# Which of the two DMA queues carries which of the first loads: one change to a fused LayerNorm, SSM and SwiGLU kernel

## The chip, the core and the metric

The kernel runs on one core of a Trainium2 chip. Its engines are TensorE (PE in the profile, with PEld for its weight loads), VectorE (DVE), ScalarE (ACT), GpSimd (POOL) and SyncE (SP). SyncE does no arithmetic here: it issues nearly all the DMAs. ScalarE issues a few at the very start. The DMAs of SyncE and those of ScalarE form two queues, and 16 DMA engines move the bytes of both. The metric is the device time of one execution in microseconds; less is better.

## The reference

The input `x` has 2048 rows of 512 bf16 values. It is normalised row by row, and the normalised rows go through two branches whose results are added to `x`:

```python
xn = _layernorm(x, axis=-1)
# branch A: a diagonal complex state-space model, state size 512
Lam_bar = jnp.exp(dt * Lam)
B_bar = ((Lam_bar - 1.0) / Lam)[:, None] * Bmat
Bu = jnp.einsum("bld,pd->blp", xn + 0j, B_bar)
# h_t = Lam_bar * h_(t-1) + Bu_t, for t = 0 .. 2047, kept as hseq
yA = 2.0 * jnp.einsum("blp,dp->bld", hseq, Cmat).real + xn * Dskip
# branch B: SwiGLU with 1376 hidden units
yB = (silu(xn @ w_gate) * (xn @ w_up)) @ w_down
return x + yA + yB
```

## The kernel before, in words

The 2048 rows are 16 tiles of 128 rows, and four tiles make a chunk; there are four chunks. The inner dimension of 512 is four K tiles of 128. For each chunk TensorE multiplies the transposed normalised rows by the gate and up weights and by the SSM input matrix; VectorE runs the recurrence as scans; in the end TensorE accumulates the down projection and the SSM output in the same banks, and VectorE adds them to `x` (`dc_pair`).

The kernel is written as a graph of tasks (`g.add`, and `dma` for transfers). A planner, `_schedule`, orders the tasks of ScalarE, VectorE and GpSimd by estimated times. Tasks of SyncE and TensorE stay in the order in which they were written (`_CHAIN`). The transfers on ScalarE's queue are chained by `order=`, so they are its first instructions. Every DMA has a semaphore of its own, and what needs its bytes waits for that semaphore.

The change is about the first microseconds, the work on chunk 0 (`ln_chunk0`, `xt_tile` and `ffn_gate_quarters`). There, everything is cut finer than later:

- Each of the four `x` tiles is loaded by a DMA of 128 KB (`x_load`), and each K tile of the first seven gate column blocks (896 of 1376 columns) by a DMA of 224 KB (`wg_load`; the names of its four DMAs end in k0 to k3).
- For each `x` tile VectorE takes the statistics (`bn_stats`, L518, and `bn_aggr`, L519), ScalarE the square root (L520), VectorE the reciprocal (L525) and the normalised tile (L501). TensorE transposes the tile into PSUM (L549), and ScalarE copies the result to SBUF in pieces (L560); VectorE does so for the last tile (L558).
- TensorE then multiplies by quarters (L764): for `x` tile 0, seven matmuls of 128 columns with K tile 0, seven with K tile 1, seven with K tile 2 and seven with K tile 3; then the same for `x` tiles 1, 2 and 3. The two transposes of the first half of `x` tile 1 stand after the fourth matmul of K tile 2. TensorE takes all this in the written order, so a K tile that is missing holds up everything behind it.
- Before the data arrive TensorE runs matmuls on a constant (`pe_warm`, L480).

SyncE's queue begins with `x` 0, `x` 1, gate k1, `x` 2, gate k3, `x` 3; then come three small parameter rows (`pload`) and the large loads of the up weights, of the remaining gate columns and of `x` tiles 4 to 7. ScalarE's queue begins with `ld_touch`, a read of 16 pairs of elements, one pair from every eighth row of gate K tile 0, whose destination `tch` nobody reads; then gate k0 and gate k2.

Of the kernel before, what the change touches and what calls it, by code (L numbers as in the profile page):

```python
# [12 lines left out]
B16 = mybir.dt.bfloat16  # L13
# [237 lines left out]
def bass_parallel_sum__ssm_conv_s5__swiglu_ffn__prompt_kernel(  # L251
# [23 lines left out]
    KT = D // 128  # L275
# [6 lines left out]
    g = _Graph()  # L282
    es = ExitStack()
    with es:
        def sb(name, shape, dt):
            return es.enter_context(nc.sbuf_tensor(name, shape, dt))
# [7 lines left out]
        x_sb = sb("x_sb", [128, NT, D], B16)  # L294
# [34 lines left out]
        st = sb("st", [128, 8, 6], F32)  # L329
# [4 lines left out]
        mhalf = sb("mhalf", [128, NT], F32)  # L334
        sd0 = sb("sd0", [128, 4], F32)
        epst = sb("epst", [128, 1], F32)
        tch = sb("tch", [16, KT, 2], B16)
        prT = sb("prT", [128, 32], B16)
        praw = prT[:].rearrange("p (a e) -> p e a", e=8)
        prow = sb("prow", [128, 32], B16)  # L340
# [48 lines left out]
        x_v = A_x[0].rearrange("(a p) d -> p a d", p=128)  # L389
        out_v = out[0].rearrange("(a p) d -> p a d", p=128)  # L390
        wg_v = B_w_gate.rearrange("(k p) f -> p k f", p=128)
# [5 lines left out]
        def dma(name, dst, src, writes, nbytes, reads=(), after=(), out_=False, eng="sp", xpose=False, prio=0.0, order=(), beside=(), **kw):  # L397
            after = tuple(after)
            if xpose:
                after = after + tuple(t for t in dma_tasks if t.name not in beside)  # L400
                fn = lambda e, dst=dst, src=src: e.dma_start_transpose(out=dst, in_=src)
                est, nb = 1900.0, int(nbytes * 1.2) + 140000
            else:
                if xp_state[0] is not None:
                    after = after + (xp_state[0],)
                fn = lambda e, dst=dst, src=src: e.dma_start(dst, src, **kw)  # L406
                est, nb = 330.0 + nbytes / 900.0, nbytes
            t = g.add(eng, fn, reads=reads, writes=writes, name=name, dma=True, after=after, out=out_, est=est, nbytes=nb, prio=prio, order=order)
            dma_tasks.append(t)
            if xpose:  # L410
                xp_state[0] = t
            return t

        TILEB = 128 * D * 2
# [7 lines left out]
        def x_load(a, **kw):  # L422
            return dma("ld_x%d" % a, x_sb[:, a:a + 1, :], x_v[:, a:a + 1, :], [("x", a)], TILEB, **kw)

        def wg_load(nm, k0, k1, **kw):
            return dma("ld_wg" + nm, wg[:, k0:k1, 0:FG], wg_v[:, k0:k1, 0:FG], [("wg", nm)], (k1 - k0) * 128 * FG * 2, **kw)

        g.add("pool", lambda e: e.memset(prow[:], 0.0), writes=[("prow0",)], name="prow0", est=100)
        x_load(0)
        x_load(1)  # L430
        act_q = [dma("ld_touch", tch[0:16, 0:1], wg_v[0:128:8, 0:1, 0:2], [("tch",)], 16 * 4, eng="act")]
        act_q.append(wg_load("k0", 0, 1, eng="act", order=(act_q[-1],)))
        act_q.append(wg_load("k2", 2, 3, eng="act", order=(act_q[-1],)))
        wg_load("k1", 1, 2)
        x_load(2)
        wg_load("k3", 3, 4)
        x_load(3)
        pload("ld_ldt", 2, A_log_dt)
# [11 lines left out]
        def loads_stage_b2():  # L450
# [11 lines left out]
              reads=[("dsk",)], writes=[("ident",)], name="ident", est=300)  # L462
        g.add("pool", lambda e: e.iota(iot[:], pattern=[[1, TP]], base=0, channel_multiplier=0, allow_small_or_imprecise_dtypes=True),
              writes=[("iot",)], name="iota", est=1000)
# [35 lines left out]
        def ln_apply(a, order=()):  # L500
            return g.add("dve", lambda e: e.tensor_scalar(out=xn_sb[:, a % NXN, :], in0=x_sb[:, a, :], scalar1=mv[:, a, 0:1], scalar2=rstd[:, a:a + 1],  # L501
                                                          op0=ALU.subtract, op1=ALU.mult),
                         reads=[("x", a), ("mv", a), ("rstd", a)], writes=[("xn", a % NXN)], name="xn%d" % a, est=350, order=order)
# [10 lines left out]
        def ln_chunk0():  # L514
            last = None
            for a in range(4):
                order = (last,) if last else ()
                last = g.add("dve", lambda e, a=a: e.bn_stats(out=st[:, a, :], in_=x_sb[:, a, :]), reads=[("x", a)], writes=[("st", a)], name="bnst%d" % a, est=640, order=order)  # L518
                last = g.add("dve", lambda e, a=a: e.bn_aggr(out=mv[:, a, :], in_=st[:, a, :]), reads=[("st", a)], writes=[("mv", a)], name="bnag%d" % a, est=160, order=(last,))  # L519
                hold["sd%d" % a] = g.add("act", lambda e, a=a: e.activation(out=sd0[:, a:a + 1], in_=mv[:, a, 1:2], func=AF.Sqrt, bias=EPS),  # L520
                                         reads=[("mv", a)], writes=[("sd0", a)], name="sd%d" % a, est=190)
                if a == 3:
                    last = g.add("dve", lambda e: e.transpose(out=prT[:], in_=prow[:]), reads=[("prow", k) for k in range(3)] + [("prow0",)],
                                 writes=[("praw", k) for k in range(3)], name="parT", est=90, order=(last,))
                last = g.add("dve", lambda e, a=a: e.reciprocal(out=rstd[:, a:a + 1], in_=sd0[:, a:a + 1]), reads=[("sd0", a)], writes=[("rstd", a)],  # L525
                             name="rstd%d" % a, est=140, order=(last,))
                last = ln_apply(a, (last,))
            hold["xn3"] = last
# [214 lines left out]
        def ffn_gate_quarters(pairs):  # L743
# [5 lines left out]
            pe_warm(8, 512, wbank)  # L749
            pe_warm(2, 128, wbank)  # L750
            ln_chunk0()
            xt_tile(0, 0, 1, wbank)
            xt_tile(0, 1, 4)
# [309 lines left out]
```

## Time and profile before

| what | us |
|---|---|
| median of three runs | 178.35 (178.0, 178.35, 180.07) |
| profiled execution, its own time | 177.91 |
| its span, from the first to the last instruction | 176.1 |
| PE busy | 172.5 (98%) |
| DVE busy | 162.0 (92%) |
| ACT busy | 83.5 (47%) |
| share of PE in the chain that ended last | 95% |
| share of DMA in that chain | 3% |

The profiled execution spends 1.8 us outside its span. The chain that ended last is followed back from the last instruction, at each step to what released it; what lies on it set the end. Busy times of other engines are no cost of their own.

These are the first DMAs, in the order of their issue. The start of the issue is from the timeline, the time from there to landing from the list of DMA issues, each asked for in a window that holds that issue alone or beside one of another tile; the last column is their sum, to 0.1 us.

| transfer | queue | issue starts | issue to landing | landed |
|---|---|---|---|---|
| touch read | ACT | 0.78 | 1.9 | 2.7 |
| x 0 | SP | 0.79 | 2.1 | 2.9 |
| gate k0 | ACT | 1.23 | 3.2 | 4.4 |
| x 1 | SP | 1.25 | 3.0 | 4.3 |
| gate k2 | ACT | 1.70 | 4.7 | 6.4 |
| gate k1 | SP | 1.71 | 4.47 | 6.18 |
| x 2 | SP | 2.18 | 4.5 | 6.7 |
| gate k3 | SP | 2.66 | 4.5 | 7.2 |
| x 3 | SP | 3.14 | 4.4 | 7.5 |

### The profile page before, as it was taken

What the parts mean: (1) busy time and instruction counts of PE and PEld (TensorE: products, weight loads), DVE (VectorE), ACT (ScalarE), POOL (GpSimd) and SP (SyncE); (2) the same over time, 40 slices, a digit from 0 to 9 for tenths busy, and PEclk for the clock granted to TensorE, in tenths of its full rate; (3) what the DMA queues carried; (4) which work ended last, traced back from release to release, by engine and by line L of the source; (5) the groups of instructions that cost most, each with busy time, mean ns of one, the idle gap of its engine ahead of it and who ended that gap; (6) DMA issues with size and microseconds to landing.
All of it is one profiled execution on the core that took longest, in us unless ns stands there. A gap on an engine that the chain in (4) does not pass through costs nothing.

```text
span 176.1 us, 2524 instructions
## 1 busy us (share of the span) xinstructions
PE 172.5 (98%) x978; PEld 84.8 (48%) x978; DVE 162.0 (92%) x279; ACT 83.5 (47%) x113; POOL 10.8 (6%) x21
## 2 busy tenths in 40 slices
PE   7899999999999999999999999999999999999995
PEld 2794444444444496444444444444444444444443
DVE  2776998899999999999999999999999999999933
ACT  4469989799999866597560000000265620000000
POOL 3040500127000000000000000000000000000000
PEclk9999999999999999999999999999999999999999
DMA  5898663566685202300411000022100000000122
GB/s 165 269 384 184 118 119 113 178 121 103 119 275 128 40 0 60 63 0 2 112 39 28 4 0 0 0 84 98 60 0 0 0 0 0 4 0 0 60 91 89
DMA packets 27143, 13.69 MB, mean 78 GB/s; under 512 B 19356, under 2 KB 27004, under 8 KB 27132
## 3 DMA queue, kind: packets, MB, share of 16 engines
q1 hardware_dynamic: 26812, 13.08, 28.6%
q10 hardware_dynamic: 320, 0.46, 0.8%
q8 instruction: 7, 0.11, 0.3%
q14 instruction: 4, 0.03, 0.1%
HBM read 6.85 MB, written 2.10 MB: 51 GB/s over the span
## 4 chain that ended last, share of the span: by engine, by line
PE 95%; DMA 3%; SPq 0%; issue 0%; DVE 0%
PE pb L721 36%; PE pb L918 20%; PE pb L932 16%; PE pb L849 16%; PE pb L764 3%; PE pb L814 3%; DMA wgu<-in_B_w_gate_dram 3%; PE pb L957 2%; SPq L406 0%; PE pb L549 0%; DVE x_sb L936 0%; PE pb L929 0%
## 5 line engine op out<-in xcount | busy, mean ns | idle before, releaser
L721 PE MATMUL pb<-xnT,wgu 128*128 128x512 bf16 x212 | 46.2, 379 | 0.0
L889 DVE TENSOR_TENSOR_SCAN rot<-sm,car,rot 128x512 bf16<-128x512 f32 x32 | 39.2, 1267 | 0.1
L733 ACT ACTIVATE sg<-pb 128x1024 bf16<-128x1024 f32 x20 | 20.1, 1022 | 39.6 <-PE pb L721 38.4
L721 PEld LDWEIGHTS pb<-xnT,wgu 128*128 128x128 bf16 x212 | 20.7, 98 | 24.8 <-ACT sg L733 0.2
L932 PE MATMUL pb<-W,hss 128*128 128x512 bf16 (+2 forms) x136 | 28.2, 367 | 0.0
L918 PE MATMUL pb<-wd,hT 128*128 128x512 bf16 (+2 forms) x130 | 26.4, 363 | 0.0
L799 ACT ACTIVATE uf<-pb 128x1024 bf16<-128x1024 f32 x20 | 20.5, 1027 | 6.4 <-PE pb L721 5.3
L849 PE MATMUL pb<-xnT,BT 128*128 128x512 bf16 x96 | 21.0, 379 | 0.0
L932 PEld LDWEIGHTS pb<-W,hss 128*128 128x128 bf16 x136 | 12.8, 98 | 15.2 <-issue 0.8
L856 ACT ACTIVATE u_sb<-pb 128x1024 bf16<-128x1024 f32 x16 | 16.4, 1023 | 5.8 <-PE pb L849 5.2
L918 PEld LDWEIGHTS pb<-wd,hT 128*128 128x128 bf16 x130 | 12.3, 98 | 14.0
L721 PE MATMUL pb<-scrC,wgu 128*128 128x512 bf16 x80 | 17.4, 379 | 0.0
L849 PEld LDWEIGHTS pb<-xnT,BT 128*128 128x128 bf16 x96 | 9.4, 98 | 11.3
L936 DVE TENSOR_TENSOR x_sb<-pb,x_sb 128x512 bf16<-128x512 f32 (+2 forms) x17 | 10.7, 644 | 4.0 <-PE pb L932 4.0
L721 PEld LDWEIGHTS pb<-scrC,wgu 128*128 128x128 bf16 x80 | 7.8, 98 | 9.2
L802 DVE TENSOR_TENSOR hT<-sg,uf 128x1024 bf16<-128x1024 bf16 x15 | 10.1, 681 | 0.1
L880 DVE TENSOR_TENSOR rot<-u_sb,cosT 128x2048 bf16<-128x2048 bf16 x8 | 9.8, 1220 | 0.5 <-ACT u_sb L856 0.5
L880 DVE TENSOR_TENSOR rot<-u_sb,sin 128x2048 bf16<-128x2048 bf16 x8 | 9.7, 1217 | 0.0
L880 DVE TENSOR_TENSOR rot<-rot,sin 128x2048 bf16<-128x2048 bf16 x8 | 9.7, 1216 | 0.0
L880 DVE TENSOR_TENSOR rot<-rot,cosT 128x2048 bf16<-128x2048 bf16 x8 | 9.7, 1210 | 0.0
L880 DVE TENSOR_TENSOR hss<-rot 128x2048 bf16<-128x2048 bf16 x8 | 9.6, 1216 | 0.0
L880 DVE TENSOR_TENSOR rot<-rot 128x2048 bf16<-128x2048 bf16 x8 | 9.6, 1216 | 0.0
(85 smaller groups left out, 159.7 us busy)
## 6 DMA issues: line engine op xcount, KB each, us to landing
out_dram<-x_sb SPq DMA_DIRECT2D x15, 128.0 KB, 1.7
x_sb<-in_A_x_dram SPq DMA_DIRECT2D x3, 512.0 KB, 4.6
wd<-in_B_w_down_dram SPq DMA_DIRECT2D x1, 1280.0 KB, 6.3
wgu<-in_B_w_up_dram SPq DMA_DIRECT2D x1, 768.0 KB, 4.9
wgu<-in_B_w_up_dram SPq DMA_DIRECT2D x1, 608.0 KB, 6.9
x_sb<-in_A_x_dram SPq DMA_DIRECT2D x4, 128.0 KB, 3.7
wgu<-in_B_w_gate_dram SPq DMA_DIRECT2D x1, 480.0 KB, 5.8
wgu<-in_B_w_gate_dram ACTq DMA_DIRECT2D x2, 224.0 KB, 4.0
```

What stands on the lines that cost most here:

```text
L721: inst = e.matmul(pbank[0:fs, bk, :].rearrange("p (j t) -> p j t", j=4), lhsT=w[:, kt, i * 128:i * 128 + fs], rhs=xnT[c][:, :, kt, :], sta ...
L733: g.add("act", lambda e: e.activation(out=sg[rows, sl, 0:n, :].rearrange("p a t -> p (a t)"), in_=pair_f32(rows, bk, 512 * n), func=AF.Sil ...
L764: inst = e.matmul(pbank[:, bk, q * 128:(q + 1) * 128], lhsT=wg[:, kt, i * 128:(i + 1) * 128], rhs=xnT[0][:, q, kt, :], start=(kt == 0), st ...
L799: g.add("act", lambda e: e.activation(out=uf[rows, ul, 0:n, :].rearrange("p a t -> p (a t)"), in_=pair_f32(rows, bk, 512 * n), func=AF.Ide ...
L802: g.add("dve", lambda e: e.tensor_tensor(out=hT_pair(c, i0), in0=sg[rows, sl, 0:n, :], in1=uf[rows, ul, 0:n, :], op=ALU.mult), reads=[("sg ...
L849: inst = e.matmul(pbank[:, bk, :].rearrange("p (j t) -> p j t", j=4), lhsT=BT[:, ri, kt, pt * 128:(pt + 1) * 128], rhs=xnT[c][:, :, kt, :] ...
L856: g.add("act", lambda e: e.activation(out=u_sb[:, us].rearrange("p r t -> p (r t)"), in_=pair_f32(slice(0, 128), b0), func=AF.Identity), r ...
L880: tt = lambda out, a, b, op, r, w, nm: g.add("dve", lambda e: e.tensor_tensor(out=out, in0=a, in1=b, op=op), reads=r, writes=w, name="%s_% ...
L889: g.add("dve", lambda e, A0=A0, A1=A1, k=k, ri=ri, pt=pt: e.tensor_tensor_scan(out=A1[:, k, ri, :], data0=rr[:, pt:pt + 1].to_broadcast([1 ...
L918: inst = e.matmul(pbank[:, bk, 0:nc_], lhsT=hT_pair(c, i - i % 2)[:, i % 2, lt * 128:(lt + 1) * 128], rhs=wd[:, i, c0:c0 + nc_], start=(i ...
L932: inst = e.matmul(pbank[:, bk, 0:nc_], lhsT=hss[:, hb, pt, ri, lt * 128:(lt + 1) * 128], rhs=W12[:, ri, pt, c0:c0 + nc_], start=False, sto ...
L936: g.add("dve", lambda e: e.tensor_tensor(out=x_sb[:, a, c0:c0 + nc_], in0=pbank[:, bk, 0:nc_], in1=x_sb[:, a, c0:c0 + nc_], op=ALU.add), r ...
```

## The change

The tile `x` 0 is loaded by two DMAs of 64 rows, the first at the head of SyncE's queue, the second at the head of ScalarE's. The read of 16 pairs and its tile `tch` are gone. Gate k0 stays second on ScalarE's queue; behind it comes `x` 2 in place of gate k2. SyncE's queue is now `x` 0 rows 0 to 63, `x` 1, gate k1, gate k2, gate k3, `x` 3, and then as before. The first `bn_stats` waits for both halves.

```diff
-        tch = sb("tch", [16, KT, 2], B16)
...
-        x_load(0)
+        dma("ld_x0", x_sb[0:64, 0:1, :], x_v[0:64, 0:1, :], [("x", 0)], TILEB // 2)
         x_load(1)
-        act_q = [dma("ld_touch", tch[0:16, 0:1], wg_v[0:128:8, 0:1, 0:2], [("tch",)], 16 * 4, eng="act")]
+        act_q = [dma("ld_x0b", x_sb[64:128, 0:1, :], x_v[64:128, 0:1, :], [("x0b",)], TILEB // 2, eng="act")]
         act_q.append(wg_load("k0", 0, 1, eng="act", order=(act_q[-1],)))
-        act_q.append(wg_load("k2", 2, 3, eng="act", order=(act_q[-1],)))
+        act_q.append(x_load(2, eng="act", order=(act_q[-1],)))
         wg_load("k1", 1, 2)
-        x_load(2)
+        wg_load("k2", 2, 3)
         wg_load("k3", 3, 4)
         x_load(3)
...
-                last = g.add("dve", lambda e, a=a: e.bn_stats(out=st[:, a, :], in_=x_sb[:, a, :]), reads=[("x", a)], writes=[("st", a)], name="bnst%d" % a, est=640, order=order)
+                last = g.add("dve", lambda e, a=a: e.bn_stats(out=st[:, a, :], in_=x_sb[:, a, :]), reads=[("x", a)] + ([("x0b",)] if a == 0 else []), writes=[("st", a)], name="bnst%d" % a, est=640, order=order)
```

The planner's estimates change with it, and two small reorderings follow between about 18 and 23 us: VectorE takes one `tzs` step (L673, 0.69 us) after the next up product's multiplication instead of before it, and ScalarE takes one cosine of four values (L614, 0.29 us) ahead of a sine table and a SiLU instead of behind them. TensorE's order is unchanged.

## The prediction

> **What bounds the kernel now.** I read the chain that ended last first, because only what lies on it can move the end. Its pieces in order of time (start, length, what) around the change:
>
> ```profile
> 1.71 4.47 DMA wgu<-in_B_w_gate_dram
> 6.18 0.14 issue
> 6.32 0.77 PE pb L764 x11
> 7.09 0.11 PE pb L549 x2
> 7.20 0.79 PE pb L764 x13
> ...
> 10.99 2.12 PE pb L764 x38
> 13.11 11.22 PE pb L721 x52
> ```
>
> From 6.32 us on the chain is TensorE alone, to 174.33. The transfer ahead of it is gate k1, issued at 1.71, landed at 6.18. Next I read the waits of TensorE over the whole span (who waited for whom: total, times, longest):
>
> ```profile
> PE pb L480 <- PEq L1048: 0.8, 1, 0.8
> PE pb L549 <- DVE xn_sb L501: 0.5, 1, 0.5
> PE pb L764 <- DMA wgu<-in_B_w_gate_dram: 0.4, 1, 0.4
> ```
>
> There are three: the program's start, the first transposes waiting for normalised tile 0, and K tile 1. After that TensorE never waits. So the change is worth what it moves the point from which TensorE runs dense, and no more, as long as nothing behind begins to wait. Third, the stretches of the beginning (from:to, length, busy time of PE, PEld, DVE, ACT and POOL with counts, granted clock, DMA share, GB/s), to see what limits the transfers:
>
> ```profile
> 2.00:3.00 1.00, 1.00 (x4) 0.38 (x3) 0.10 (x1) 0.81 (x1) 0.15 (x4) 1.00 0.88 209
> 3.00:4.00 1.00, 1.00 (x5) 0.32 (x4) 0.77 (x2) 0.93 (x3) 0.00 (x0) 1.00 1.02 340
> 4.00:5.00 1.00, 0.51 (x8) 0.34 (x6) 0.89 (x3) 0.04 (x1) 0.00 (x0) 1.00 0.99 357
> 5.00:6.00 1.00, 0.82 (x11) 0.42 (x8) 0.66 (x4) 0.90 (x4) 0.00 (x0) 1.00 1.04 376
> 6.50:7.50 1.00, 1.00 (x21) 0.94 (x19) 0.81 (x2) 0.26 (x2) 0.00 (x0) 1.00 0.75 104
> 7.50:8.50 1.00, 1.00 (x22) 1.00 (x19) 0.69 (x4) 0.67 (x4) 0.00 (x0) 1.00 0.85 263
> 8.50:9.50 1.00, 1.00 (x21) 0.97 (x19) 0.88 (x3) 0.29 (x3) 0.00 (x0) 1.00 1.05 389
> ```
>
> From 3 to 6 us the 16 DMA engines are full at 340 to 376 GB/s. So the order of the bytes decides when a tile lands. And there are two slow stretches: 2 to 3 us, when `x` and `w_gate` are read for the first time, and 6.5 to 8.5, when `w_up` is.
>
> **When TensorE could be dense.** A matmul of 128 columns takes 0.056 us (2.12 / 38). The first with data starts at 5.35, seven with k0 last to 5.74; k1 then took until 6.18, plus 0.14 to the first matmul. From 6.32 come 7 with k1 and 4 with k2, 2 transposes, 3 with k2, and the first with k3 at 7.20 + 3 x 0.056 = 7.37. Gate k3 lands at 7.2. So two limits coincide: without the wait for k1, TensorE would have stood at k3, until 7.2 + 0.14 = 7.34.
>
> **The change, part by part.**
>
> *Order of the gate tiles and of `x` 2.* I count the KB that both queues have moved when a tile is complete, taking turns as they did before (both k1 and k2, each behind about as many bytes on its own queue, landed at 6.2 and 6.4).
> - k1 before: 480 on SP (x 0, x 1, k1) and 448 on ACT (k0, k2), 928. After: 416 and 416 (half of x 0, k0, x 2), 832. At 360 GB/s the 96 KB are 0.27 us: 5.9 instead of 6.18.
> - k2 before: the same 928, landed 6.4. After: 640 + 416 = 1056, so 0.36 us later, 6.75.
> - k3 before: 832 + 448 = 1280. After: 864 + 416 = 1280. Nothing.
> - x 2 before: 608 + 448 = 1056, landed 6.7. After: 832, 0.6 us earlier.
>
> With those times TensorE starts k1 at 6.05, has done its seven at 6.44, waits for k2 until 6.75 + 0.14 = 6.89, and does 4 matmuls, 2 transposes and 3 matmuls (0.50 us) until 7.39. Against 7.37 that is nothing: what k1 gains, k2 gives back, and k3 is where it was. I count **0.0**.
>
> *The halves of `x` 0.* Each brings a wait for `bn_stats`; behind it on VectorE stand the whole tile 0 chain, and behind that TensorE. The halves move the same 128 KB on the same engines; issues of 0.41 (SP) and 0.42 us (ACT, the touch read) start at 0.79 and 0.78 now. Landed 2.9 before; I bound it by 0.2 us either way: 128 KB take 0.37 us at 360 GB/s, and half of that can be won if the queues start side by side, or lost if x 1, now behind 64 rows only, runs beside the second half. From its landing to the first matmul are 2.45 us, to 5.35; even 5.55 leaves seven k0 matmuls done at 5.94, ahead of the k1 that lands at 5.9 plus 0.14. So **0.0**. The Trainium skill, page "DMA: Bandwidth & Descriptors", section "Rules for kernel authors", says of two transfers to disjoint partition halves that they serialise on the same engines, so that one transfer should be used; by it the halves land no sooner than 2.9, against it 0.2 sooner, and the sum is 0.0 by both. No row here shows a tile loaded in halves.
>
> *The small read.* As an instruction it is replaced by the second half's issue, so ScalarE's table load still starts at about 2.19 us. What it did to the bytes is unknown: it was the first read of `w_gate`. Its upper end comes from `w_up`, which nothing touches before: 104 and 263 GB/s in the two stretches of 1 us against 389 afterwards are 0.73 + 0.32 = 1.05 us lost. The lower end is below nothing: x 1 and k0 ran beside the touch read in the stretch of 209 GB/s, 0.4 us short of the 340 that followed, and if the read itself was a part of that, some 0.1 comes back. I take **+0.3**, near the start of this same program (0.4 lost, with `x` and `w_gate` cold together), and keep -0.1 and +1.0. Nothing hides it: k3 stands at the end of what is late.
>
> *The lag of one engine.* The trace's landing records show each transfer by its 16 engines. For k1, 15 had landed at 5.50 and the last at 6.18; for k3, 15 at 6.49 and the last at 7.21. It is one engine, late since one packet of k1 took 914 ns (from 3.41 us) where the others take 74. For x 0, x 1 and k0 the last was 0.02 to 0.15 us behind the 15th. Whether the next execution has such a packet I can't see. Without it TensorE is bound by itself and by normalised tile 1 (L501 ends at 6.39): transposes at 6.45, two of 0.11 us together, 3 matmuls, k3 at 6.73, which is 0.64 earlier. A repeat costs nothing more. Taken in the middle: **-0.3**; ends -0.64 and +0.6, the latter a second such packet.
>
> *Behind it.* Tile 2: `bn_stats` waited for x 2 until 6.66; now it can start at 6.39 behind L501, so normalised tile 2 is done at 8.18 instead of 8.45, and the transposes stand at 8.81, at the earliest 8.17. x 3 keeps its place (1408 KB) and landed 0.8 us before it was read. The rest of the gate columns landed at 11.8 (issue at 6.04 plus 5.8) and are needed at 13.1. The two small reorderings on VectorE and ScalarE are hidden: the hidden states for the first output pass end at 100.9 and TensorE takes them at 110.44, and at the end VectorE waits 4.0 us for TensorE (L936).
>
> **Sum.** 0.0 + 0.0 + 0.3 - 0.3 = 0.0 against the profiled execution's 177.91 (span 176.1 and 1.8 around it). That execution is 0.44 below the median of the runs, 178.35; the runs that I forecast scatter like those. I forecast 178.3, between -0.5 and +0.5 of it.
>
> **The rivals.**
> 1. *The lag does not come again and the first read costs little.* Then k3 no longer holds TensorE, and the dense run starts 0.5 to 0.64 earlier: 177.7. For it: 15 of 16 engines were in time, and x 2 is early. Against it: the same 1280 KB stand ahead of k3. 0.22.
> 2. *Slower: the first read of `w_gate` moves into gate k0.* Each engine's first packet of 1792 bytes now pays what a 4-byte packet paid, and the engines hold up both queues. It decides as soon as it costs more than the lag gives back, 0.3 us; at the price of `w_up`, +1.0 with a middling lag, it is +0.7, 179.05. For it: the stretch at 6.5. Against it: w_up's load names four K tiles in each partition, so it opens more places at once than k0. 0.24.
> 3. *Slower: the clock.* The eight warming matmuls of 512 columns and two of 128 took 3.44 us, 0.79 ns a column; L721 takes 215.8 ns for 512 columns, 0.42. (The clock column says 1.00 in both.) Were TensorE to fall back for some 3.4 us, that is 1.7 us more: 180.05. It would take far more idle time than the 0.5 and 0.4 us that it waited with a warm array. 0.04. The Trainium skill, page "TensorE: Matmul & The Clock Gate", section "Part 1: The HAM clock gate", has the clock fall after an idle window of about 3.4 us; by that even a k0 late by 1 us keeps it, and nothing in this trace shows a fall.
> 4. *The change does not do what it says*, that is, x 0 lands no sooner: this is inside the forecast, since x 0 sets nothing.
>
> **How the numbers follow.** Forecast 0.50, rivals 0.22, 0.24 and 0.04. The range goes from 177.5 (rival 1 with 0.2 of scatter) to 179.3 (rival 2 with its upper end); it leaves out rival 3 and the chance that the median falls on a run like the 180.07. About 2% (3.6 us) is what a measurement of this kernel can tell from no change, and no case reaches it: same 0.97, faster 0.01, slower 0.02.
>
> **What would show it.** In the changed kernel: k3's landing near 7.2 and the last wait of TensorE now for k2 or k3 instead of k1; x 2 landed by 6.1 and no wait of the third `bn_stats`; x 0 landed at 2.7 to 3.1; the first matmul of L721 at 13.1, give or take 0.5. Rival 2 would show as a stretch from 2.5 to 4 us well below 340 GB/s and k0 landing after 5. I am wrong if any wait of TensorE appears after 8 us, or if x 0 sets the start.

## The result, and the profile after

| | before | changed |
|---|---|---|
| median of 14 runs, us | 177.82 (177.43 to 180.07) | 178.29 (178.11 to 179.56) |
| ratio, with 95% interval | | 1.0045 (1.0032 to 1.0059) |
| profiled execution, us | 177.91 | 179.5 |
| its span | 176.1 | 177.7 |
| busy time of PE in it | 172.5 | 174.3 |

The change costs 0.45%, a little under 0.5 us in the median. The forecast of 178.3 lies beside the median of 178.29, but by luck. It was a forecast of no change, made against a median of 178.35 that rested on three runs, one of them stray; with 14 runs the kernel before has 177.82. The loss is real, and none of the forecast's steps had it. Three later runs of the kernel before, at 180.09 to 180.28 with a mean granted clock of 0.99 instead of 1.00, are left out of the comparisons below.

The runs of the changed kernel fall into two groups: ten at 178.11 to 178.68, four at 179.17 to 179.56. The profiled execution is one of the four. First its chain that ended last, pieces in order of time (start, length, what):

```profile
0.78 2.67 DMA x_sb<-in_A_x_dram
...
3.55 0.70 DVE st L517
...
5.40 0.61 PE pb L548 x4
...
6.22 1.94 PE pb L763 x18
...
8.37 1.22 PE pb L763 x13
...
12.58 2.12 PE pb L763 x38
14.70 11.22 PE pb L720 x52
```

Two things differ from before. The chain no longer comes in through gate k1 but through `x` 0, whose first half lands at 0.78 + 2.67 = 3.45 us instead of 2.9; behind it the first `bn_stats` starts at 3.55 instead of 2.90. And the 18 matmuls of 128 columns from 6.22 take 1.94 us, 0.107 us each, where the last 38 take 0.056 each: TensorE's clock was still at half its rate. The waits of TensorE over the span (total, times, longest) say the same:

```profile
PE pb L479 <- PEq L1047: 0.8, 1, 0.8
PE pb L548 <- DVE xn_sb L500: 0.8, 1, 0.8
```

The wait for a gate tile is gone and the wait for normalised tile 0 has grown from 0.5 to 0.8 us. Why `x` 0 is late is seen in the timeline of the DMA issues (start, length, queue), SyncE's first and then ScalarE's:

```profile
0.78 1.47 SPq L405 DMA_DIRECT2D x_sb<-in_A_x_dram  x2
2.30 1.38 SPq L405 DMA_DIRECT2D wgu<-in_B_w_gate_dram  x3
...
0.80 0.56 ACTq L405 DMA_DIRECT2D x_sb<-in_A_x_dram  x1
1.39 0.59 ACTq L405 DMA_DIRECT2D wgu<-in_B_w_gate_dram  x1
2.01 0.45 ACTq L405 DMA_DIRECT2D x_sb<-in_A_x_dram  x1
```

Before, the first two issues of SyncE took 0.88 us together and gate k1 was issued at 1.71. Now they take 1.47 (0.60 and 0.81 by the single records), and gate k1, and everything behind it on that queue, is issued 0.6 us later. ScalarE's first two take 0.56 and 0.59 instead of 0.42 and 0.45. The stretches of the beginning (columns as in the prediction) show that the transfers fall behind at the same time:

```profile
2.00:3.00 1.00, 1.00 (x4) 0.39 (x3) 0.00 (x0) 0.50 (x1) 0.15 (x4) 1.00 0.86 176
3.00:4.00 1.00, 1.00 (x4) 0.36 (x3) 0.45 (x1) 0.99 (x2) 0.00 (x0) 1.00 0.80 263
4.00:5.00 1.00, 0.61 (x3) 0.15 (x1) 0.66 (x4) 0.29 (x2) 0.00 (x0) 1.00 1.06 381
5.00:6.00 1.00, 0.60 (x5) 0.45 (x5) 0.96 (x3) 0.28 (x1) 0.00 (x0) 1.00 0.98 308
```

From 2 to 4 us 439 KB are moved; before it was 549. The column of the granted clock says 1.00 all along, also where matmuls of 128 columns take 0.107 us, so here the clock has to be read from the durations.

Behind this beginning nothing changed. The time of an execution is the start of the first L721 matmul on the chain (L720 in the changed kernel) plus 164.8 us: 13.11 and 177.91 before, 14.70 and 179.5 after. In the executions that I compare below it is 164.8 to 165.0. So a kernel's whole difference can be read from that one start.

### The profile page after: what moved, and what is told of

Same layout as the page of the kernel before. It is cut to its first block, busy times and chain, and to the rows that moved or that the text cites. A ratio compares the mean times of both kernels' runs of the same rounds, so it can differ in the third digit from the quotient of the medians.

```text
span 177.7 us, 2524 instructions
## 1 busy us (share of the span) xinstructions
PE 174.3 (98%) x978; PEld 86.6 (49%) x978; DVE 162.0 (91%) x279; ACT 83.5 (47%) x113; POOL 9.6 (5%) x21
## 4 chain that ended last, share of the span: by engine, by line
PE 96%; DMA 1%; DVE 1%; issue 0%; ACT 0%; DVEq 0%
PE pb L720 35%; PE pb L917 19%; PE pb L931 16%; PE pb L848 16%; PE pb L763 4%; PE pb L813 3%; PE pb L956 2%; DMA x_sb<-in_A_x_dram 1%; PE pb L548 1%; DVE st L517 0%; DVE xn_sb L500 0%; DVE x_sb L935 0%; PE pb L479 0%; ACT sd L519 0%; DVE mv L518 0%
## 5 line engine op out<-in xcount | busy, mean ns | idle before, releaser
L720 PE MATMUL pb<-xnT,wgu 128*128 128x512 bf16 x212 | 46.2, 379 | 0.0
L720 PEld LDWEIGHTS pb<-xnT,wgu 128*128 128x128 bf16 x212 | 20.7, 98 | 24.8 <-ACT sg L732 0.2
L855 ACT ACTIVATE u_sb<-pb 128x1024 bf16<-128x1024 f32 x16 | 16.4, 1024 | 5.8 <-PE pb L848 5.2
L720 PE MATMUL pb<-scrC,wgu 128*128 128x512 bf16 x80 | 17.4, 379 | 0.0
L720 PEld LDWEIGHTS pb<-scrC,wgu 128*128 128x128 bf16 x80 | 7.8, 98 | 9.2
```

Source lines behind the costliest of these rows:

```text
L720: inst = e.matmul(pbank[0:fs, bk, :].rearrange("p (j t) -> p j t", j=4), lhsT=w[:, kt, i * 128:i * 128 + fs], rhs=xnT[c][:, :, kt, :], sta ...
L855: g.add("act", lambda e: e.activation(out=u_sb[:, us].rearrange("p r t -> p (r t)"), in_=pair_f32(slice(0, 128), b0), func=AF.Identity), r ...
```

## The experiments

The first theory: the halves are to blame, since DMAs of 64 rows are slow to issue. The rivals: the missing small read, the order of the gate tiles, and TensorE's clock by itself. The kernels up to "The halves alone" take the change apart.

### The halves taken back

Against the changed kernel:

```diff
-        dma("ld_x0", x_sb[0:64, 0:1, :], x_v[0:64, 0:1, :], [("x", 0)], TILEB // 2)
+        x_load(0)
...
-        act_q = [dma("ld_x0b", x_sb[64:128, 0:1, :], x_v[64:128, 0:1, :], [("x0b",)], TILEB // 2, eng="act")]
-        act_q.append(wg_load("k0", 0, 1, eng="act", order=(act_q[-1],)))
+        act_q = [wg_load("k0", 0, 1, eng="act")]
```

> The changed kernel with x 0 loaded whole again, by one DMA of 128 rows at the head of SyncE's queue; ScalarE's queue is gate k0, x 2. Theory (the halves are to blame: with them the first two issues took 0.60 and 0.81 us on SyncE and 0.56 and 0.59 on ScalarE instead of 0.41 to 0.45, and x 0 landed at 3.45 instead of 2.87): SyncE's first issues take 0.41 again, x 0 lands at 2.9, and the time is that of the kernel before or 0.1 to 0.3 us less, 177.5 to 177.9. Rival (the missing small read: gate k0 is now the first to read w_gate): k0 lands at 4.7 or later, and the time stays at 178.1 to 178.4.

Measured: 179.66 us (179.48 to 180.25, 5 runs), ratio to before 1.0115 (1.0097 to 1.0132). Neither was right: taking the halves back makes it 1.4 us worse than the changed kernel. SyncE's issues take 0.41 again, as expected, but `x` 0 lands at 4.03, later than ever. Gate k0 is not slow: it lands at 3.84, 0.6 us earlier than before. It now starts at the same moment as `x` 0, and the two share the DMA engines (the packets are counted further down).

### The order alone

```diff
-        act_q.append(wg_load("k2", 2, 3, eng="act", order=(act_q[-1],)))
+        act_q.append(x_load(2, eng="act", order=(act_q[-1],)))
         wg_load("k1", 1, 2)
-        x_load(2)
+        wg_load("k2", 2, 3)
```

> The kernel before with the order alone changed: x 2 on ScalarE's queue behind gate k0, gate k1, k2, k3 in a row on SyncE's; x 0 whole and the small read kept. Theory: nothing in the mean (k3 stands behind the same 1280 KB), 177.6 to 178.0. Rival (the order costs, since k2 is later): 178.1 to 178.4, with TensorE's wait at k2.

Measured: 177.63 us (177.36 to 178.06, 12 runs), ratio 0.9998 (0.9987 to 1.0009). The order is worth nothing, as the sum of bytes had it, though not tile by tile: in the profiled execution k1 landed at 5.12 and k2 at 6.01, where the sum had 5.9 and 6.75, and the chain comes in through `x` 0 (2.98).

### The small read alone

```diff
-        act_q = [dma("ld_touch", tch[0:16, 0:1], wg_v[0:128:8, 0:1, 0:2], [("tch",)], 16 * 4, eng="act")]
-        act_q.append(wg_load("k0", 0, 1, eng="act", order=(act_q[-1],)))
+        act_q = [wg_load("k0", 0, 1, eng="act")]
```

> The kernel before without the small read alone. Theory (the halves are to blame): at most 0.1 us more than before, 177.7 to 178.0, k0 landed by 4.6. Rival (the first read of w_gate costs in k0): 178.2 to 178.8, k0 landed after 4.7, and packets of 1792 bytes of k0 slow on most engines.

Measured: 178.59 us (178.54 to 179.63, 6 runs), ratio 1.007 (1.0046 to 1.0094). The rival's time, but not by its mechanism: k0 lands at 4.1, earlier than before. The list of DMA issues, in a window that holds the first issue of either queue (KB, us from issue to landing):

```profile
wgu<-in_B_w_gate_dram ACTq DMA_DIRECT2D x1, 224.0 KB, 3.3
x_sb<-in_A_x_dram SPq DMA_DIRECT2D x1, 128.0 KB, 3.1
```

`x` 0 takes 3.1 us instead of 2.1. Its tile 0 chain then sets the start, as the last lines ahead of the dense stretch in the chain of this kernel show:

```profile
0.78 3.10 DMA x_sb<-in_A_x_dram
...
6.36 1.18 PE pb L762 x18
...
13.59 11.22 PE pb L719 x52
```

### Where the small read reads

If the small read is worth 1 us because it keeps gate k0 back, it may read anything.

```diff
-        act_q = [dma("ld_touch", tch[0:16, 0:1], wg_v[0:128:8, 0:1, 0:2], [("tch",)], 16 * 4, eng="act")]
+        act_q = [dma("ld_touch", tch[0:16, 0:1], x_v[0:128:8, 0:1, 0:2], [("tch",)], 16 * 4, eng="act")]
```

> The kernel before with the small read taken from x tile 0 instead of w_gate, the same 16 pairs of 4 bytes. If the small read is worth what it is because it holds gate k0 back while x 0 lands: x 0 lands at 2.9 and the time is that of before, 177.5 to 177.8. If it is worth it because it reads w_gate first: packets of k0 are slow (300 to 500 ns on most engines), k0 lands at 4.7 or later, and the time is 178.0 to 178.6.

Measured: 177.82 us (177.38 to 178.65, 12 runs), ratio 1.0000 (0.9981 to 1.0018); `x` 0 lands at 2.95, k0 at 4.30. So the small read is a spacer: it puts off the issue of gate k0 by 0.45 us, and until its bytes come `x` has the engines without the gate. The packets show it. Those of `x` have 1024 bytes, those of the gate tiles 1792 (896 columns). Of the packets begun before 2.4 us, the kernel before has 116 of `x` and none of the gate, this kernel 124 and none; without the small read there are 48 and 26, with the halves taken back 7 and 31. That the small read reads `w_gate` first is worth nothing that can be measured.

### Both halves on one queue

Against the changed kernel: the second half goes to SyncE's queue, behind the first.

```diff
+        dma("ld_x0b", x_sb[64:128, 0:1, :], x_v[64:128, 0:1, :], [("x0b",)], TILEB // 2)
         x_load(1)
-        act_q = [dma("ld_x0b", x_sb[64:128, 0:1, :], x_v[64:128, 0:1, :], [("x0b",)], TILEB // 2, eng="act")]
-        act_q.append(wg_load("k0", 0, 1, eng="act", order=(act_q[-1],)))
+        act_q = [wg_load("k0", 0, 1, eng="act")]
```

> The changed kernel with both halves of x 0 on SyncE's queue, one behind the other; ScalarE's queue is gate k0, x 2. If a DMA of 64 rows is slow to issue in itself: SyncE's first two issues take 0.55 to 0.6 us each, x 0 lands at 3.3 or later, and the time is 178.2 or more. If it is the two queues' starting side by side with such DMAs: the issues take 0.41, x 0 lands by 3.1 (one issue of 0.45 later at most), and the time is 177.7 to 178.1.

Measured: 180.86 us (180.07 to 181.67, 6 runs), ratio 1.0181 (1.0155 to 1.0207). The timeline of its DMA issues, SyncE and then ScalarE:

```profile
0.79 1.86 SPq L405 DMA_DIRECT2D x_sb<-in_A_x_dram  x3
2.70 0.96 SPq L405 DMA_DIRECT2D wgu<-in_B_w_gate_dram  x2
...
0.78 0.38 ACTq L405 DMA_DIRECT2D wgu<-in_B_w_gate_dram  x1
```

Three issues in 1.86 us: both halves take 0.6 us each, and so does `x` 1 behind them. ScalarE's 128-row load beside them takes 0.38. So a second queue is not needed for the slow issue; it goes with the 64-row DMAs. `x` 0 lands at 4.69, 1.2 us later than in the changed kernel: its second half is issued only at 1.44, and gate k0 runs beside the first. TensorE idles 2.3 us for it, and in this trace the granted clock is seen to fall (columns as in the prediction):

```profile
6.00:7.00 1.00, 0.44 (x5) 0.28 (x5) 0.96 (x3) 0.17 (x1) 0.00 (x0) 1.00 0.80 278
8.00:9.00 1.00, 1.00 (x12) 1.00 (x11) 0.96 (x3) 0.00 (x0) 0.00 (x0) 0.50 0.84 144
```

It stands at 0.50 from 7.09 to 10.51 us, and the matmuls of 128 columns take 0.107 us there.

### Halves of 128 rows

Against the changed kernel: the same two queues and places, but halves of 256 columns.

```diff
-        dma("ld_x0", x_sb[0:64, 0:1, :], x_v[0:64, 0:1, :], [("x", 0)], TILEB // 2)
+        dma("ld_x0", x_sb[:, 0:1, 0:256], x_v[:, 0:1, 0:256], [("x", 0)], TILEB // 2)
-        act_q = [dma("ld_x0b", x_sb[64:128, 0:1, :], x_v[64:128, 0:1, :], [("x0b",)], TILEB // 2, eng="act")]
+        act_q = [dma("ld_x0b", x_sb[:, 0:1, 256:512], x_v[:, 0:1, 256:512], [("x0b",)], TILEB // 2, eng="act")]
```

> The changed kernel with x 0 in two halves of 256 columns (all 128 rows, 512 bytes each) instead of two halves of 64 rows, at the same places. Theory (a DMA of 64 rows takes 0.6 us to issue instead of 0.41 and starts late; that is what the halves cost): the first two issues take 0.40 to 0.45 us on both queues, x 0 lands at 2.7 to 3.0, and the time is 177.4 to 177.8, that of the kernel before or a little less. Rival (two queues that start with the same tile hold each other up): issues of 0.55 or more or x 0 at 3.3 or later, 178.1 to 178.4.

Measured: 177.72 us (177.54 to 178.34, 12 runs), ratio 0.9989 (0.9966 to 1.0013). The same lines of its timeline:

```profile
0.79 0.89 SPq L405 DMA_DIRECT2D x_sb<-in_A_x_dram  x2
1.72 1.38 SPq L405 DMA_DIRECT2D wgu<-in_B_w_gate_dram  x3
...
0.78 0.40 ACTq L405 DMA_DIRECT2D x_sb<-in_A_x_dram  x1
```

Issues are back at 0.4 us and the loss is gone. `x` 0 lands at 3.15, a little outside what I expected and 0.3 later than as one DMA, so halving the tile wins nothing even in this form; but the second half is a spacer as good as the small read. With this the loss of the changed kernel is pinned to the 64-row form.

### The halves alone

The kernel before, with the 64-row halves at the heads of the queues and the small read behind the second:

```diff
-        x_load(0)
+        dma("ld_x0", x_sb[0:64, 0:1, :], x_v[0:64, 0:1, :], [("x", 0)], TILEB // 2)
         x_load(1)
-        act_q = [dma("ld_touch", tch[0:16, 0:1], wg_v[0:128:8, 0:1, 0:2], [("tch",)], 16 * 4, eng="act")]
+        act_q = [dma("ld_x0b", x_sb[64:128, 0:1, :], x_v[64:128, 0:1, :], [("x0b",)], TILEB // 2, eng="act")]
+        act_q.append(dma("ld_touch", tch[0:16, 0:1], wg_v[0:128:8, 0:1, 0:2], [("tch",)], 16 * 4, eng="act", order=(act_q[-1],)))
```

> The kernel before with the halves of 64 rows alone: second half at the head of ScalarE's queue, the small read behind it, then gate k0 and k2; order on SyncE's queue as before. Theory (the changed kernel loses by its 64-row halves, and the missing small read costs nothing there because the second half holds gate k0 back in its place): x 0 lands at 3.4, 178.0 to 178.5, as the changed kernel. Rival (the missing small read, as the first read of w_gate, is a part of the changed kernel's loss): 177.6 to 177.9.

Measured: 178.87 us (178.12 to 180.15, 8 runs), ratio 1.0064 (1.0032 to 1.0095): four runs at 178.12 to 178.39, four at 179.35 to 180.15. The lower four are where the changed kernel's lower group is, so the halves carry the whole loss. A side cost of this kernel is one more issue on ScalarE: its table load ends at 4.24 and the first square root waits for it.

### The two groups: TensorE's clock

In the profiled executions of the upper group (changed kernel 179.5, halves alone 179.35, halves taken back 179.63) the matmuls of 128 columns take 0.107 us until about 9 us. Between the warming matmuls and the first transposes TensorE idled 0.8, 0.7 and 1.3 us in these three. In two others the warming matmuls also ran at half rate to their end, but `x` 0 landed at 2.95 to 2.98 and the idle time was 0.2 to 0.3 us (the order alone, and the last kernel below): there the full rate came at 6.7 and 6.2. One execution speaks against a plain rule: without the small read TensorE idled 1.1 us and had the full rate from 5.8.

The kept traces hold more on this than the column shows: the moments at which a change of the granted clock was recorded, in eight of the executions. The first rise stands at 3.54 to 4.02 us in four (the kernel before, halves of 256 columns, both halves on one queue, the changed kernel run again below), at 6.70 and 6.21 in the two others just named, at 8.98 and 9.00 in the halves taken back and the halves alone. With both halves on one queue three changes lie 3.41 us apart. So I take it that the clock is settled for stretches of 3.41 us whose start differs from execution to execution. The stretches that end in a rise had TensorE at work for at least 2.7 us of the 3.41 (80%, with halves of 256 columns; counted from the starts and widths of its matmuls), the full stretches ahead of a late rise for at most 2.5 (72%, in the order alone and the halves alone). An idle time of 1 us matters, then, where it falls into the stretch that decides. The execution without the small read would fit, if its stretch ended soon after the warming matmuls; it has no such record. This is a reading of eight executions and not an experiment.

The next three kernels change the warming matmuls only, by one line:

```diff
-            pe_warm(8, 512, wbank)
+            pe_warm(5, 512, wbank)
```

> The kernel before with five warming matmuls of 512 columns instead of eight; every DMA as before. Theory of the clock (the gap between the warming matmuls and the first transposes decides how often matmuls still take 107 ns after 6.5 us): the gap grows from 0.5 to about 1.6 us with x 0 landing at 2.9 all the same, and at least a third of the runs lie 1 to 2 us above the others, at 178.8 or more. Rival (the upper group comes from late data, not from TensorE's idle time): all but a stray run at 177.3 to 178.3.

This is the kernel before, with every DMA as it was. Measured: 179.19 us (178.44 to 180.42, 6 runs), ratio 1.008 (1.0054 to 1.0106). Three runs lie at 178.44 to 178.74 and three at 179.64 to 180.42; none is left where the kernel before has its median. From the timeline of TensorE in the profiled execution (180.42):

```profile
6.95 1.33 PE L764 MATMUL pb<-xnT,wgu 128*128 128x128 bf16 x11 [0.53 <-DMA wgu<-in_B_w_gate_dram]
8.08 0.42 PE L549 MATMUL pb<-ident,xn_sb 128*128 128x128 bf16 x2
8.29 1.59 PE L764 MATMUL pb<-xnT,wgu 128*128 128x128 bf16 x13
```

Before, the 11 and the 13 matmuls took 0.77 and 0.95. Less work for TensorE ahead of the data makes the kernel slower by more than a microsecond, with no DMA moved. (In this execution gate k1 also landed late, at 6.81.)

The changed kernel with more warming matmuls, ten and then twelve:

> The changed kernel with ten instead of eight warming matmuls of 512 columns. Theory of the clock (in the changed kernel's profiled execution matmuls of 128 columns took 107 ns until 9.3 us, since TensorE idled from 4.4 to 5.4; its runs fall into a group at 178.1 to 178.7 and one at 179.2 to 179.6): with that gap closed the upper group is gone, matmuls take 56 ns from 7 us at the latest, median 177.9 to 178.3. Rival (the clock's rise does not depend on the gap): about 3 runs in 10 stay above 179.

Measured: 178.3 us (178.06 to 179.44, 11 runs), ratio 1.0034 (1.0013 to 1.0055). Nine of 11 runs are at 178.06 to 178.61, two above 179. That is between theory and rival.

> The changed kernel with twelve warming matmuls of 512 columns instead of eight; cold, they last until 6.1 us, past the first transposes at 5.4. Theory of the clock: no run in the upper group, all at 178.0 to 178.6, no lower than the changed kernel's lower group, since gate k2 and k3 land no sooner (6.9 and 7.5). Rival (late data make the upper group): runs above 179 as often as before, 2 to 4 in 12.

Measured: 178.59 us (178.02 to 178.66, 5 runs), ratio 1.0047 (1.0031 to 1.0063). No run in the upper group, but five runs are few, and the warming matmuls now last until 6.0 us and hold up the transposes themselves.

> The changed kernel once more, unchanged, for a profile of its lower group. Theory: with the clock up before 6.5 us, TensorE runs dense from the landing of gate k2 or k3 (6.9 to 7.5 us, issued 0.6 us later than before), the first matmul of 512 columns on the gate weights starts at 13.2 to 13.6, and the execution takes 164.8 us more, 178.0 to 178.4; 2 to 4 runs in 12 lie above 179. Rival: TensorE is held by normalised tile 0 or 2 instead, with the gate tiles landed before they are needed.

Measured: 178.25 us (178.06 to 178.44, 9 runs), ratio 1.0029 (1.0019 to 1.0039). Not one run in the upper group this time. Over all sessions the changed kernel has 4 of 23 runs above 179, the kernel before 2 of 89. So the upper group comes by chance, and that the change brings it more often is likely but not settled; the 0.5 us of the lower group is there without it. That group's chain:

```profile
5.89 0.97 PE pb L763 x14
6.86 0.10 issue
6.96 0.38 PE pb L763 x4
...
13.31 11.22 PE pb L720 x52
```

The clock is up here. 14 matmuls with k0 and k1 start at 5.89. At 0.056 us each the next, the first with k2, could follow at 6.67, but it stands until 6.96 (the chain shows only 0.10 of this, since it models the ends of matmuls). Gate k2 was issued at 2.77 and landed at 6.83 by the landing records. With ten warming matmuls, whose time is also that of the lower group, the chain itself comes in through this tile:

```profile
2.30 0.43 SPq L405
...
2.77 4.13 DMA wgu<-in_B_w_gate_dram
6.91 0.14 issue
7.04 0.38 PE pb L763 x4
```

So in the lower group it is gate k2 that holds TensorE; `x` 0 comes 0.5 us late too, but with 0.3 us to spare. With halves of 256 columns, in the same order, k2 was issued at 2.19 and landed at 6.20. The later issue is only a part of the difference: against that kernel the changed one has moved 54 KB less from 2 to 5 us, and another 123 KB less from 5 to 6 us (258 against 381), when k1, k2 and k3 have all been issued. From 5 to 6 us the six profiled executions with 64-row halves moved 258 to 334 KB, the eight without them 341 to 387. What slows that stretch no run here shows.

### Gate k3 ahead of `x` 2

The kernel before with gate k3 ahead of `x` 2:

```diff
-        x_load(2)
         wg_load("k3", 3, 4)
+        x_load(2)
```

> The kernel before with gate k3 ahead of x 2 on SyncE's queue, for a time below both kernels. k3 stands behind 1152 KB instead of 1280 and lands 0.3 us sooner, x 2 0.6 us later. If k3 is what holds TensorE in the mean: 177.3 to 177.6. If TensorE's own pace and the chain of tile 1 hold it by then, or tile 2 comes late: 177.6 to 178.0.

Measured: 177.65 us (177.52 to 178.14, 11 runs), ratio 1.0003 (0.9991 to 1.0014). Gate k3 lands at 6.16, ahead of its need, and nothing is won: the chain then comes in through `x` 0, which lands at 2.95, and the 2.5 us of normalising behind it. I found no version below the kernel before.

## Why the prediction was wrong

- **What bounds the kernel, and that nothing behind the beginning would wait: right.** The constant 164.8 us from the first L721 matmul to the end of the execution holds in every chain compared.
- **Order of the gate tiles and of `x` 2, 0.0: right.** 0.9998 for the order alone. The step also had k2 as the tile that would hold TensorE. In the changed kernel it does (6.83 measured, 6.75 forecast), but not for the bytes ahead of it: with the order alone k2 landed at 6.01 and held nothing.
- **"The halves of `x` 0", 0.0 with 0.2 us either way: the step that failed.** It took the issue of a half at 0.41 and 0.42 us, the row of a 128-row load and that of the small read. Measured are 0.60 and 0.56, with 0.81 and 0.59 for the loads right behind them. `x` 0 lands 0.5 to 0.6 us later, outside the bounds, and in the profiled execution it sets the start, which the prediction named as a sign of being wrong. What the step did not look at is the rest of the queue: every later issue on SyncE moves by 0.6 us, and k2 lands 0.6 us later than with halves of 256 columns. In the lower group this late k2 is the 0.5 us of the result; the slow stretch from 5 to 6 us has its part in it. The nearest rows were rows of other shapes; that a shape could change the price of an issue did not occur to me. The Trainium skill's page "DMA: Bandwidth & Descriptors", section "Rules for kernel authors", with its one 128-partition transfer in place of two partition halves, was the better guide to the outcome. Its reason, that halves share the same engines, is not what decided: halves of 256 columns share them too and lost nothing.
- **"The small read", +0.3 for a first read of `w_gate`: wrong in its mechanism.** Read from `x`, it is worth the same (ratio 1.0000). It is a spacer that keeps gate k0 from sharing the engines with `x` 0; without any spacer the loss is 1.0 us (1.007). In the changed kernel the second half takes its place, so the term should have been 0. Rival 2 was built on it and falls with it. Its slow packets did come: of the 1792-byte packets begun before 3.3 us, 13 took over 0.3 us in the changed kernel, at most one where the small read of `w_gate` stood ahead (their median is 0.07). But k0 landed at 4.39, no later than before, and the halves alone keep that read and lose the same.
- **"The lag of one engine", -0.3: a relief that the change could not bring.** The lag comes and goes with the execution: for k1 the last engine was 0.73 us behind the 15th in the halves taken back and in the read from `x`, 0.55 without the small read, 0.01 to 0.02 in the order alone, halves of 256 columns and k3 first. And 177.91 lies 0.1 to 0.35 us above the medians of the kernel before in the five sessions (177.56 to 177.82), so a relief counted against it is none against a median. My +0.3 and -0.3 cancelled; both should have been 0, and the 0.5 us stood in the step that I had put at 0.
- **Rival 3, the clock: near in size, wrong in kind and in its threshold.** Upper runs lie 1.2 us above the others, near the 1.7 that I priced. But I priced a fall, and held that it took far more idle time than 0.5 us. In the upper executions the clock does not fall, it rises late, and 0.7 to 1.3 us of idle time go with that. A fall is seen once, with 2.3 us of idle time (both halves on one queue). That is less than the idle window of about 3.4 us that the prediction has from the Trainium skill, and the measurement decides. The Trainium skill's page "TensorE: Matmul & The Clock Gate", Part 1, has the clock rise after a busy window of about 3.4 us; the eight traces with clock records agree, with changes 3.41 us apart and no rise after a stretch in which TensorE was at work for 72% of the time or less.

What stays open: why a 64-row DMA is slow to issue and slows the one behind it, why fewer bytes move from 5 to 6 us in its company, and how often the upper group comes with the changed kernel.

## What to carry to other kernels

A DMA is not priced by its bytes alone: look in a trace for the issue time of that very shape, and count what it does to every issue behind it on its queue. What looks like a useless small transfer at the head of a second queue may be the spacer that lets the critical load have the DMA engines first; ask of every removed transfer what starts earlier because of it. And before a difference of some tenths of a microsecond is forecast, the profiled execution has to be placed among many runs, since its own accidents are as large as the terms.

## What the runs showed that I had not expected

- Issues of 64-row loads took 0.55 to 0.60 us on either queue, those of 128-row loads at the same place 0.38 to 0.41; the 128-row load right behind two 64-row ones on SyncE's queue took 0.59, behind one such load, with ScalarE's half beside it, 0.81.
- Gate k0 (224 KB) at the head of one queue beside `x` 0 (128 KB) at the head of the other moves the landing of `x` 0 from 2.9 to 3.9 or 4.0 us. Position in a second queue is a matter of 1 us.
- TensorE's matmuls ran at half rate until 9.3 us in one execution and from 5.3 us on at full rate in another of the same kernel, with the granted clock given as 1.00 in both.
- Two of 89 runs of the kernel before lie above 179 (179.97 and 180.07), and none in three of the five sessions.
